# One product of a Strassen-style transform, made for two column chunks at once by a second Strassen level

## The chip, the core and the metric

The kernel runs on one core of one Trainium2 chip. A core has five engines with a queue each: TensorE (PE in the profile; its weight loads are listed as PEld), VectorE (DVE), ScalarE (ACT), GpSimd (POOL) and SyncE (SP, which here only starts transfers). Transfers between the chip's main memory (DRAM) and the on-chip memory (SBUF) are started from SP's or POOL's queue and carried by 16 DMA engines. Matmul results go to PSUM, eight banks of 128 partitions by 512 fp32 numbers. The metric is the device time of one execution in microseconds (us).

## The reference

`x` has 2048 rows of 640. It is normalised by row (`xn`), and two branches are made from it: a Fourier mix over both axes, and a gated feed-forward block, whose result gates the mix.

```python
xn = _layernorm(x, axis=-1)
a = jnp.einsum("bsd,ed->bse", xn, dft_hid_re)
b = jnp.einsum("bsd,ed->bse", xn, dft_hid_im)
s = jnp.einsum("ts,bse->bte", dft_seq_re, a) - jnp.einsum("ts,bse->bte", dft_seq_im, b)
g = _silu((_silu(xn @ w_gate) * (xn @ w_up)) @ w_down)
return x + s * g
```

The kernel swaps the order of the two transforms: it first forms `dft_seq_re @ xn` and `dft_seq_im @ xn` (the sequence transform, 2048 x 2048 by 2048 x 640), keeps them in DRAM (`p_dram`), and then applies the hidden transform. The change is in the sequence transform.

## The kernel before

**Precision.** Every matmul operand in fp32 is split into a high part (ScalarE, a copy rounded to the matmul's format) and a low part (VectorE, the difference). `split` (line 328) records both; `mm3` (line 354) makes one product as three matmuls, high by high, high by low and low by high.

**Strassen.** Every large product is done by one level of Strassen's scheme (Winograd's form): the left matrix in four blocks 11, 12, 21, 22, the right in four, seven products p1, p5, p6, p2, p3, p7, p4 instead of eight. The 640 columns of `xn` are 2 x 256 that go through the scheme and 128 more that are multiplied directly; these ride on operands that are there anyway (d1, d2, d3).

**The sequence transform.** `seq(k)` (line 742) is called for k = 0 to 3. k % 2 chooses real or imaginary (`ri`), k // 2 chooses `j`. A part k makes the output's row chunks of 512 numbered j (upper half) and j + 2 (lower half): in the transposed layout that the kernel uses, these are columns, hence "column chunks". So the lower half's chunks 2 and 3 belong to parts j = 0 and j = 1 of the same `ri`. The DFT matrix (`cs`) is the moving operand, 512 wide; sums of blocks of `xn` (`right`, line 642) are the weights, 128 x 128. Each product has a depth of 1024, which is 8 k-tiles, taken in four groups of two (g = 0 to 3). `run` (line 798) makes one product: for two PSUM banks, and for a third one (`dbank`) where a direct product rides along.

Left operands: `load` (line 759) brings a block of 512 KB by SP's queue, `accumulate` (line 765) adds another block onto it during the transfer by POOL's queue, `add` (line 769) adds on VectorE. `result` (line 835) reads a bank pair, adds or subtracts a kept partial result, and sends it to `p_dram` by POOL's queue. Part 0 has its own opening, which makes p1 for parts 0 and 1 at once. The order of the other parts is p1, p2, p5, p6, p3, p7, p4; part 1 starts with p2. The last product is (lines 976 to 985):

```python
run(("p4", p4, (), (2, 3)))
result("d2", (dbank[2],), None, None)
run(("p4", lambda g: last[g], b2, None))
result(21, b2, s1 if shared else None, ALU.add)
```

p4 multiplies block 22 of the DFT matrix with the weight sum nt4 (`right("p4", g, ...)`), and d3 the same block with nt5. Both sums are made once, in part 0, and kept in SBUF until the end of part 3.

**What sets the order.** The kernel doesn't issue as it goes: every operation is recorded in a plan (`Plan`, line 98), which gives the matmul steps fixed times (`step`, 0.22667 us per matmul), then evictions behind them (`post`), and sets everything that prepares operands (`prod`) backwards from its due time into the free time of its engine. The issue order of each engine is the order of these planned times. Then `place` (line 197) gives every buffer an address in one of three areas of SBUF: `hl` (split operands, 86 KB per partition), `raw` (unsplit data, 80 KB) and a third that is turned over later (20 KB). A buffer may reuse space only of one that is done by the issue order; `fit` (line 247) prefers space that has been free for some time, and takes less (`pauses`) where there is none. All waits between engines follow from the buffers. In the profile all instructions bear line 82, the recording helper, so they are told apart by their operands and shapes.

After the sequence transform come `hid_s` (hidden transform), `gate_up` and `down` (feed-forward).

Of the kernel before, what the change touches and what calls it, by code (L numbers as in the profile page):

```python
# [11 lines left out]
AF = mybir.ActivationFunctionType  # L12
ALU = mybir.AluOpType

P = 128
S, D, F = 2048, 640, 1536
TC = 512
# [80 lines left out]
class Plan:  # L98
# [98 lines left out]
    def place(self, limits, last):  # L197


        self.ops.sort(key=lambda o: o[:2])  # L200
        life = {}
        for i, (t, _, _, names, end) in enumerate(self.ops):
            for n in names:
                if n in self.size:
                    v = life.setdefault(n, [t, i, end, i])
                    v[2:] = max(end, v[2]), i
        where = {}
        turn = max(v[3] for n, v in life.items() if self.size[n][0] == "raw2")
        free = max(v[2] for n, v in life.items() if self.size[n][0] == "raw2")
        back = next(i for i, o in enumerate(self.ops) if o[0] >= self.back)  # L210
        for arena, limit in limits.items():
            wall = {"hl": [(limit, limit + last[0], turn, free + 1, 1e9), (limit + last[0], limit + sum(last), turn, free + 1, back)],
                    "raw": [(limit, limit + last[1], back, self.back + 2, 1e9)]}.get(arena, [])
            limit = max([limit, *(w[1] for w in wall)])
            mine = [(n, self.size[n][1], *v) for n, v in life.items() if self.size[n][0] == arena]
            orders = (
                lambda m: (m[2], m[3]),
                lambda m: (m[4] - m[2] < 60, m[2], m[3]),
                lambda m: (m[4] - m[2] < 60, -m[1], m[3]),
                lambda m: (-m[1], m[3]),  # L220
                lambda m: (m[2] - m[4], m[3]),
            )
            pauses = (8, 6, 4, 3, 2, 1, 0, -1, -2, -4, -8)
            tries = ((pauses[a:], o) for a in range(len(pauses)) for o in orders)
            found = [f for f in (self.fit(sorted(mine, key=o), limit, p, wall) for p, o in tries) if f]
            for long, w in [(x, y) for x in (40, 60, 80) for y in (50, 70, 100, 140)]:
                order = sorted(mine, key=lambda m: (m[4] - m[2] < long, m[2] - m[1] / w, m[3]))
                found += [f for f in (self.fit(order, limit, pauses[a:], wall) for a in range(6)) if f]
            for w in range(25, 425, 25) if not found else ():
                order = sorted(mine, key=lambda m: (m[4] - m[2] < 60, m[2] < w, m[2], m[3]))  # L230
                found += [f for f in (self.fit(order, limit, pauses[a:], wall) for a in range(len(pauses))) if f]
            if not found:
                raise ValueError(f"{arena}: no room")
            best = min(found, key=lambda f: f[0])
# [12 lines left out]
    @staticmethod  # L247
    def fit(mine, limit, pauses, wall):

        placed, where, cost = [], {}, {}  # L250
        for n, size, ta, ia, tb, ib in mine:
            near = sorted((o, e, xa, ja, xb, jb) for o, e, xa, ja, xb, jb in placed
                          if (ja <= ib and ia <= jb) or (xa < tb + 8 and ta < xb + 8))
            near += [(a, a if i < ia and t < ta and ib < j else e, ta, ia, tb, ib) for a, e, i, t, j in wall]
            near.sort()
            for pause in pauses:
                gaps, at = [], 0
                for o, e, xa, ja, xb, jb in near:
                    if (ja <= ib and ia <= jb) or (xa < tb + pause and ta < xb + pause):
                        if o - at >= size:  # L260
                            gaps.append((o - at, at))
                        at = max(at, e)
                if limit - at >= size:
                    gaps.append((limit - at, at))
                if gaps:
                    break
            else:
                return None
            o = min(gaps)[1]
            where[n] = o  # L270
            for a, e, xa, ja, xb, jb in near:
                if a < o + size and o < e:
                    cost[n] = cost.get(n, 0.0) + max(0.0, 5 - (ta - xb if ta >= xa else xa - tb)) ** 2
            placed.append((o, o + size, ta, ia, tb, ib))
        return sum(cost.values()), where, cost, mine
# [3 lines left out]
def tile_fnet_swiglu(  # L279
# [97 lines left out]
    def wide(ap):  # L377
        return ap.rearrange("p (a b) -> p a b", b=TC)
# [258 lines left out]


    p_dram = dram.tile([2, NC, ND, P, TC], F32, name="p_dram")
    sums = {}  # L640

    def right(p, g, lead):


        def quad(h, c, w=256):
            k = 8 * h + 4 * g
            return (lambda a=0, n=4: xn_tiles(k + a, n, 256 * c, w)), [(xn, i, c) for i in range(k, k + 4)]

        def new(what, a, b, op, w=256):
            if (what, g) not in sums:  # L650
                name = pl.buf((what, g), "raw", 4 * w)
                view = lambda a=0, n=4: raw(name).rearrange("p (a b) -> p a b", b=w)[:, a:a + n]
                pl.prod(lead, lambda: nc.vector.tensor_tensor(view(), a[0](), b[0](), op=op), [*a[1], *b[1]], [(name, 0)])
                sums[what, g] = view, [(name, 0)]
            return sums[what, g]

        if p == "p1":
            return quad(0, 0)
        if p == "p2":
            return quad(1, 0)  # L660
        if p == "p3":
            return quad(1, 1)
        if p == "p5":
            return new("nt1", quad(0, 0), quad(0, 1), ALU.subtract)
# [12 lines left out]
        return quad(int(p[1]) - 1, 2, P)  # L677
# [64 lines left out]
    def seq(k):  # L742
# [26 lines left out]
        def add(dst, src, lead):  # L769
            pl.prod(lead, lambda: nc.vector.tensor_tensor(raw(dst), raw(dst), raw(src), op=ALU.add),  # L770
                    [(src, 0)], [(dst, 0)])
# [171 lines left out]
            return s  # L943

        def p3(g):
            add(R[g], load(12, g, 20), 12)
            return operand("p3", g, R[g])

        def product_2():
            run(("p2", p2, b1, (1, 2)))  # L950
            result(11, b1, s1, ALU.subtract)
            result("d1", (dbank[1],), ahead["d1"] if shared else None, ALU.add)

        if fresh:
            opening()
        elif not shared:
            run(("p1", p1, b2, (1, 1)))
        s1 = ahead["s1"] if shared else copy("s1", b2)
        if not fresh:
            product_2()  # L960
        run(("p5", p5, b3, (2, 1)))
        n5 = copy("n5", b3)
        if fresh:
            product_2()
        run(("p6", p6, b2, None))
        if shared:
            u2 = pl.buf(("u2", k), "raw", 2 * TC)
# [5 lines left out]
        result(12, b3, u2, ALU.subtract)  # L973
        run(("p7", lambda g: operand("p7", g, Y[g]), b2, None))
        result(22, b2, n5, ALU.subtract)
        last = []

        def p4(g):
            last.append(operand("p4", g, load(22, g, 20)))
            return last[-1]  # L980

        run(("p4", p4, (), (2, 3)))
        result("d2", (dbank[2],), None, None)
        run(("p4", lambda g: last[g], b2, None))
        result(21, b2, s1 if shared else None, ALU.add)

    seq.n = 0


# [435 lines left out]
```

## Time and profile before

| | |
|---|---|
| median of 3 runs | 969.31 us (969.18 to 969.34) |
| profiled execution: span from first to last instruction | 967.6 us |
| its time outside the span | not listed; the median is 1.7 us above the span |
| TensorE busy | 961.5 us (99%) |
| VectorE busy | 734.5 us (76%) |
| ScalarE busy | 488.8 us (51%) |
| moved by transfers | 186.50 MB, mean 193 GB/s |
| mean granted TensorE clock | 0.999 |

How to read it: busy times are sums of an engine's instructions. Matmuls are pipelined, so a matmul's record is longer than the distance between two of them. A row of a group of instructions has line, engine, operation, output <- input, shapes, count, then busy time and mean ns of one, then the idle time of the engine just ahead of these instructions and what ended it. `hl` are split operands, `raw` unsplit data, `ps` PSUM, `xn` the normalised rows, `in_cs` the DFT matrix. The clock is given in parts of full speed. By the counts of matmuls (132 for the opening with its weights and 360 for the rest of part 0, 360 for part 1, 432 each for parts 2 and 3) part 0 ends at some 121.7 us, part 1 at 203.4, part 2 at 301.4 and part 3 at 399.4 us.

### The profile page before, as it was taken

To read this page: it belongs to the slowest core of one execution; us is meant where nothing else is said; L and a number is where in the kernel's file an instruction comes from. 1 tells how busy PE (TensorE), PEld (TensorE's weight loads), DVE (VectorE), ACT (ScalarE), POOL (GpSimd) and SP (SyncE) were. 2 spreads that over 40 slices of the span, in tenths; PEclk is the share of its full clock that TensorE was granted. 3 is DMA by queue.
4 is the path that set the end of the run, shared out by engine and by line. 5 is a ranking of instruction groups with operands and counts; after the bars stand their busy time and mean duration, and the time that the engine had idled before them with its cause. 6 is when DMAs were issued, how large, how long until landed. Compare 5 with 4: busy or idle time off the path is not lost.

```text
span 967.6 us, 11522 instructions
## 1 busy us (share of the span) xinstructions
PE 961.5 (99%) x4235; PEld 792.1 (82%) x4235; DVE 734.5 (76%) x932; ACT 488.8 (51%) x676; POOL 121.4 (13%) x185
## 2 busy tenths in 40 slices
PE   9999999999999999999999999999999999999998
PEld 5888888888888888888888888888888888888886
DVE  7889668757774687675987898999978666666775
ACT  6686445454545455544356555563446444444341
POOL 0450211011101110111100211210002000000000
PEclk9999999999999999999999999999999999999999
DMA  9997848484838497778563374449799330105793
GB/s 344 280 259 215 227 154 233 150 270 111 226 109 260 108 235 263 204 198 258 165 210 131 142 264 155 168 142 289 219 293 272 80 136 1 55 1 163 243 346 128
DMA packets 64056, 186.50 MB, mean 193 GB/s; under 512 B 6528, under 2 KB 10368, under 8 KB 64000
## 3 DMA queue, kind: packets, MB, share of 16 engines
q1 hardware_dynamic: 45952, 125.45, 39.2%
q0 software_dynamic: 18048, 60.32, 24.0%
q8 instruction: 33, 0.54, 0.2%
q14 instruction: 23, 0.19, 0.1%
HBM read 151.39 MB, written 34.36 MB: 192 GB/s over the span
## 4 chain that ended last, share of the span: by engine, by line
PE 99%; DVE 0%; DMA 0%; ACT 0%; issue 0%; DVEq 0%; ACTq 0%
PE ps L82 99%; DMA xn<-in_x 0%; DVE raw L82 0%; DVE bst L82 0%; DVE sm L82 0%; ACT raw L82 0%; ACT sm L82 0%; DVE mv L82 0%; DVEq L82 0%; ACTq L82 0%
## 5 line engine op out<-in xcount | busy, mean ns | idle before, releaser
L82 PE MATMUL ps<-hl 128*128 128x512 f32 (+1 forms) x3258 | 779.8, 388 | 0.0
L82 PEld LDWEIGHTS ps<-hl 128*128 128x128 f32 x3258 | 610.0, 188 | 126.4 <-ACT hl L82 0.2
L82 DVE TENSOR_TENSOR hl<-raw,hl 128x1024 fp32r<-128x1024 f32 (+5 forms) x360 | 346.6, 994 | 134.5 <-ACT hl L82 94.8
L82 ACT ACTIVATE hl<-raw 128x1024 fp32r<-128x1024 f32 (+6 forms) x416 | 325.1, 826 | 170.6 <-DVE raw L82 84.1
L82 PE MATMUL ps<-hl,hl 128*128 128x512 f32 (+1 forms) x954 | 259.9, 388 | 0.0
L82 ACT ACTIVATE raw<-ps 128x512 f32<-128x512 f32 (+1 forms) x144 | 98.0, 681 | 231.1 <-PE ps L82 225.0
L82 PEld LDWEIGHTS ps<-hl,hl 128*128 128x128 f32 x954 | 178.9, 188 | 36.9
L82 DVE TENSOR_TENSOR raw<-raw 128x1024 f32<-128x1024 f32 (+7 forms) x216 | 178.7, 850 | 19.6 <-ACT raw L82 15.4
L82 DVE TENSOR_TENSOR raw<-ps,raw 128x512 f32<-128x512 f32 (+1 forms) x95 | 77.3, 814 | 48.5 <-PE ps L82 47.7
L82 ACT ACTIVATE hl<-xn 128x1024 fp32r<-128x1024 f32 (+3 forms) x61 | 42.2, 724 | 13.7 <-PE ps L82 9.2
L82 DVE TENSOR_TENSOR raw<-raw,raw 128x512 f32<-128x512 f32 (+3 forms) x50 | 44.2, 892 | 6.5 <-ACT raw L82 4.3
L82 POOL DMA_DIRECT2D p_dram<-raw x24 | 16.4, 687 | 251.5 <-DVE raw L82 215.9
L82 ACT ACTIVATE raw<-raw 128x512 f32<-128x512 f32 (+1 forms) x30 | 21.6, 719 | 46.7 <-DVE raw L82 46.7
L82 DVE TENSOR_TENSOR hl<-xn,hl 128x1024 fp32r<-128x1024 f32 (+3 forms) x50 | 40.8, 833 | 4.0 <-PE ps L82 3.9
L82 POOL DMA_DIRECT2D raw<-in_cs x36 | 32.5, 985 | 57.6 <-DMA raw<-in_cs 28.7
L82 DVE SCALAR_TENSOR_TENSOR hl<-raw,hl 128x256 fp32r<-128x256 f32 (+4 forms) x56 | 32.8, 587 | 4.0 <-ACT hl L82 4.0
L82 POOL DMA_DIRECT2D out<-raw x10 | 6.9, 691 | 225.0 <-DVE raw L82 198.2
L82 POOL DMA_DIRECT2D d_p<-hl x28 | 15.2, 544 | 71.3 <-ACT hl L82 59.2
L82 ACT ACTIVATE xn<-xn,sm,rowst 128x640 f32<-128x640 f32 (+1 forms) x16 | 14.2, 909 | 4.9 <-DVE sm L82 1.8
L82 DVE BATCH_NORM_STATS2 bst<-xn 128x6 f32<-128x320 f32 x32 | 13.7, 479 | 3.6 <-DMA xn<-in_x 3.6
L82 POOL DMA_DIRECT2D y_dram<-raw x12 | 8.2, 684 | 64.6 <-DVE raw L82 46.2
L82 POOL DMA_DIRECT2D raw<-in_xt x6 | 6.9, 1297 | 72.1 <-DVE raw L82 72.1
(43 smaller groups left out, 88.0 us busy)
## 6 DMA issues: line engine op xcount, KB each, us to landing
raw<-in_cs SPq DMA_DIRECT2D x84, 512.0 KB, 7.3
hl<-d_p SPq DMA_DIRECT2D x56, 384.0 KB, 4.7
raw<-in_cs POOLq DMA_DIRECT2D x36, 512.0 KB, 9.8
raw<-in_wb SPq DMA_DIRECT2D x24, 640.0 KB, 4.6
d_p<-hl POOLq DMA_DIRECT2D x28, 384.0 KB, 3.9
p_dram<-raw POOLq DMA_DIRECT2D x16, 512.0 KB, 4.1
raw<-p_dram SPq DMA_DIRECT2D x8, 768.0 KB, 8.2
xn<-in_x SPq DMA_DIRECT2D x16, 320.0 KB, 9.8
```

Source lines behind the costliest of these rows:

```text
L82: return real(*args, **kw)
```

## The change

Parts 0 and 1 (j = 0) no longer make p4 and d3. They keep what p7 leaves in its bank pair (U3, two banks; in part 1 with s1 added) and the direct sum (D2, one bank) in SBUF. Parts 2 and 3 (j = 1) make p2 first, then `second()`, then p1, p5, p6, p3 and p7, without a p4.

`second()` makes p4 and d3 for chunks 2 and 3 of one `ri` together: block 22 of both chunks is one matrix of depth 1024 by 1024 columns, and nt4 is 1024 by 256. It is cut in four again and multiplied by seven products of depth 512 (4 k-tiles), one bank each, in the order p1, p5, p6, p2, p3, p7, p4. The direct products d1 (beside p1 and p5), d2 (beside p2) and d3 (beside p4) ride along as before. Its weights are sums of nt4's blocks (l1 to l4) and of nt5's (e, l6); its left operands are loaded by SP (`take`), added to by accumulating transfers of POOL (`grow`) and by one addition on VectorE (for p6). Chunk 2's results Z1, Z2 and Z5 are finished here from U3 and D2 and sent to `p_dram`; chunk 3's stay as W1 and in the bank `dbank[2]`, and are added in when part 2 or 3 ends.

nt4 and nt5 are made anew in parts 2 and 3 and no longer kept from part 0. In part 1 p3's left operand is added to by an accumulating transfer instead of a load and an addition. The search for buffer addresses gets a further way of ordering, used where the others find no room.

The diff, cut to its core:

```diff
 (Plan.place)
+            for o in orders if not found else ():
+                for p in (-2, 1, 3):
+                    order = sorted(mine, key=o)
+                    for _ in range(200):
+                        f = self.fit(order, limit, [x for x in pauses if x <= p or x > 5], wall)
+                        if f:
+                            found.append(f)
+                            break
+                        i = next(i for i, m in enumerate(order) if m[0] == Plan.stuck)
+                        order.insert(i // 2, order.pop(i))
...
 (right)
-                name = pl.buf((what, g), "raw", 4 * w)
+                name = pl.buf((what, g, len(turn)), "raw", 4 * w)
...
 (seq)
         def p3(g):
-            add(R[g], load(12, g, 20), 12)
+            if shared:
+                accumulate(R[g], 12, g, 14)
+            else:
+                add(R[g], load(12, g, 20), 12)
             return operand("p3", g, R[g])
...
+        def second():
+            q1, (q2, q3), d0 = b2[0], b3, b2[1]
+            Y, R = {}, {}
+            for what in [w for w in sums if w[0] in ("nt4", "nt5")]:
+                del sums[what]
+            turn.append(k)
+            nt = [right("p4", b, 16) for b in range(2)]
+            e = [right("d3", b, 16) for b in range(2)]
...
+            def grow(name, a, b, g, lead):
+                pl.prod(lead, lambda: nc.gpsimd.dma_start(wide(raw(name)), block(a, b, g), accum_op=ALU.add),
+                        [], [(name, 0), (name, 1)], 8)
...
+            def left(p, g):
+                if p == "p1":
+                    Y[g] = take(0, 0, g, 24)
+                    return Y[g]
+                if p == "p5":
+                    R[g] = take(1, 0, g, 30)
+                    grow(R[g], 1, 1, g, 22)
+                    return R[g]
+                if p == "p6":
+                    add(R[g], Y[g], 12)
+                    return R[g]
+                if p == "p2":
+                    return take(0, 1, g, 20)
+                if p == "p3":
+                    grow(R[g], 0, 1, g, 14)
+                    return R[g]
+                return Y[g] if p == "p7" else take(1, 1, g, 20)
+
+            def weights(p):
+                dst = pl.buf(("V", k, p), "hl", 8 * P)
+                src, keys = T2[p]
+                split(11, dst, 4 * P, src, keys, scale=-1.0 if p == "p1" else None, low_lead=9)
+                return dst
+
+            mix("l1", q(0, 0), q(0, 1), ALU.subtract)
+            mix("l2", q(1, 1), l["l1"], ALU.add)
+            mix("l3", q(0, 1), q(1, 1), ALU.subtract, q(0, 1))
+            mix("l4", q(1, 0), l["l2"], ALU.subtract)
+            mix("l6", e[1], e[0], ALU.subtract)
...
+            def phase(p, bank, direct=None):
...
+                for g in range(2):
+                    if (p, g) not in ops2:
+                        name = left(p, g)
+                        ops2[p, g] = o = pl.buf(("S2", k, p, g), "hl", 4 * TC)
+                        split(10, o, 2 * TC, lambda name=name: raw(name), [(name, 0), (name, 1)], low_lead=8)
+                        if p == "p6":
+                            grow(Y[g], 1, 0, g, 11.5)
...
+                    for r, bk in t[::-1]:
+                        for i in range(2):
+                            steps.append((bk, lambda part, r=r, a=2 * g + i: hl(made2[r], part, a * P, P),
+                                          lambda part, o=ops2[p, g], i=i: hl(o, part, i * TC, TC), is_first(bk)))
...
+            phase("p1", q2, ("d1", d0))
+            v1 = less("v1", q2, U3[ri], 0)
+            phase("p5", q3, ("d1", dbank[2]))
+            m5 = pl.buf(("m5", k), "raw", TC)
+            evict(m5, (q3,))
+            phase("p6", q2)
+            v2 = less("v2", q2, U3[ri], TC)
+            phase("p2", q1, ("d2", d0))
+            out(less("Z1", q1, v1, 0), 0, 1)
+            out(less("Z5", d0, D2[ri], 0, ALU.add), 4, 1)
+            phase("p3", q3)
+            out(less("Z2", q3, v2, 0), 1, 1)
+            phase("p7", q2)
+            W1 = pl.buf(("W1", k), "raw", 2 * TC)
+            pl.post(lambda: nc.vector.tensor_tensor(raw(W1, TC, TC), ps[:, q2, :], raw(m5), op=ALU.subtract),
+                    [("ps", q2), (m5, 0)], [(W1, 0)])
+            phase("p4", q2, ("d3", dbank[2]))
+            pl.post(lambda: nc.scalar.activation(raw(W1, 0, TC), ps[:, q2, :], AF.Copy), [("ps", q2)], [(W1, 0)])
...
         if fresh:
             opening()
-        elif not shared:
+        else:
+            run(("p2", p2, b1, (1, 2)))
+        if j:
+            W1 = second()
             run(("p1", p1, b2, (1, 1)))
...
+        if not j:
+            D2[ri] = pl.buf(("D2", ri), "raw", TC)
+            evict(D2[ri], (dbank[2],), after=1)
         run(("p6", p6, b2, None))
...
         run(("p7", lambda g: operand("p7", g, Y[g]), b2, None))
         result(22, b2, n5, ALU.subtract)
-        run(("p4", p4, (), (2, 3)))
-        result("d2", (dbank[2],), None, None)
-        run(("p4", lambda g: last[g], b2, None))
-        result(21, b2, s1 if shared else None, ALU.add)
+        if j:
+            result("d2", (dbank[2],), None, None)
+            result(21, b2, W1, ALU.add)
+            return
+        U3[ri] = pl.buf(("U3", ri), "raw", 2 * TC)
+        if shared:
+            combine(U3[ri], b2, s1, ALU.add, after=3)
+        else:
+            evict(U3[ri], b2, after=3)
```

More of the change, by code (lines that the diff above doesn't have):

```diff
@@ L267, in fit @@
             else:
+                Plan.stuck = n
                 return None
@@ L639, in tile_fnet_swiglu @@
     p_dram = dram.tile([2, NC, ND, P, TC], F32, name="p_dram")
-    sums = {}
+    sums, turn = {}, []
     def right(p, g, lead):
@@ L945, in p3, with block, take, mix @@
         def p3(g):
-            add(R[g], load(12, g, 20), 12)
+            if shared:
+                accumulate(R[g], 12, g, 14)
+            else:
+                add(R[g], load(12, g, 20), 12)
             return operand("p3", g, R[g])
-        def product_2():
-            run(("p2", p2, b1, (1, 2)))
+        def second():
[6 more added lines that the diff above has]
+            e = [right("d3", b, 16) for b in range(2)]
+            q = lambda b, c: (lambda: nt[b][0]()[:, :, c * P:c * P + P], nt[b][1])
+            l = {}
+            def block(a, b, g):
+                return cs[a + 2, ri, 2 + b, :, 2 * g:2 * g + 2]
+            def take(a, b, g, lead):
+                seq.n += 1
+                name = pl.buf(("c", seq.n), "raw", 2 * TC)
+                pl.prod(lead, lambda: nc.sync.dma_start(wide(raw(name)), block(a, b, g)), [], [(name, 0), (name, 1)])
+                return name
+            def grow(name, a, b, g, lead):
+                pl.prod(lead, lambda: nc.gpsimd.dma_start(wide(raw(name)), block(a, b, g), accum_op=ALU.add),
+                        [], [(name, 0), (name, 1)], 8)
+            def mix(what, a, b, op, over=None):
+                if over is None:
+                    name = pl.buf((what, k), "raw", 4 * P)
+                    over = (lambda: raw(name).rearrange("p (a b) -> p a b", b=P)), [(name, 0)]
+                l[what] = over
+                pl.prod(12, lambda: nc.vector.tensor_tensor(over[0](), a[0](), b[0](), op=op), [*a[1], *b[1]], over[1])
+            def left(p, g):
[25 more added lines that the diff above has]
+            mix("l6", e[1], e[0], ALU.subtract)
+            T2 = {"p1": q(0, 0), "p5": l["l1"], "p6": l["l2"], "p2": q(1, 0), "p3": q(1, 1),
+                  "p7": l["l3"], "p4": l["l4"], "d1": e[0], "d2": e[1], "d3": l["l6"]}
+            made2, ops2, todo = {}, {}, []
+            def phase(p, bank, direct=None):
+                t = [(p, bank)] if bank is not None else []
+                if direct:
+                    t.append((direct[0], direct[1]))
+                at = pl.now
+                for g in range(2):
+                    pl.now = at + g * 6 * len(t) * MM
+                    if (p, g) not in ops2:
[4 more added lines that the diff above has]
+                            grow(Y[g], 1, 0, g, 11.5)
+                    for r, _ in t:
+                        if r not in made2:
+                            made2[r] = weights(r)
+                pl.now = at
+                for g in range(2):
+                    steps, reads = [], []
+                    for r, bk in t[::-1]:
+                        for i in range(2):
+                            steps.append((bk, lambda part, r=r, a=2 * g + i: hl(made2[r], part, a * P, P),
+                                          lambda part, o=ops2[p, g], i=i: hl(o, part, i * TC, TC), is_first(bk)))
+                    for r, _ in t:
+                        reads += both(made2[r])
+                    product(steps, list(dict.fromkeys(both(ops2[p, g]) + reads)))
+            def out(name, e0, n):
+                pl.post(lambda: nc.gpsimd.dma_start(p_dram[ri, 2, e0:e0 + n].rearrange("k p t -> p k t"), wide(raw(name))),
+                        [(name, 0)], [("pd", ri, 2)], 5, 8)
+            def less(what, bank, other, a, op=ALU.subtract):
+                name = pl.buf((what, k), "raw", TC)
+                pl.post(lambda: nc.vector.tensor_tensor(raw(name), ps[:, bank, :], raw(other, a, TC), op=op),
+                        [("ps", bank), (other, 0)], [(name, 0)])
+                return name
+            phase("p1", q2, ("d1", d0))
[16 more added lines that the diff above has]
+            pl.post(lambda: nc.scalar.activation(raw(W1, 0, TC), ps[:, q2, :], AF.Copy), [("ps", q2)], [(W1, 0)])
+            for bank in (q1, q2, q3, d0):
+                first.pop(bank)
+            return W1
@@ L951, in product_2, with result_1 @@
+        def result_1():
             result(11, b1, s1, ALU.subtract)
@@ L959, in seq @@
         if not fresh:
-            product_2()
+            result_1()
         run(("p5", p5, b3, (2, 1)))
@@ L963, in seq @@
         if fresh:
-            product_2()
+            run(("p2", p2, b1, (1, 2)))
+            result_1()
+        if not j:
+            D2[ri] = pl.buf(("D2", ri), "raw", TC)
+            evict(D2[ri], (dbank[2],), after=1)
         run(("p6", p6, b2, None))
@@ L975, in seq @@
         result(22, b2, n5, ALU.subtract)
[L976 to L980, printed above, removed]
-        run(("p4", p4, (), (2, 3)))
-        result("d2", (dbank[2],), None, None)
-        run(("p4", lambda g: last[g], b2, None))
-        result(21, b2, s1 if shared else None, ALU.add)
+        if j:
[7 more added lines that the diff above has]
+            evict(U3[ri], b2, after=3)
+    U3, D2 = {}, {}
     seq.n = 0
```

## The prediction

> **What bounds the kernel now.** The page's head was read first, then the chain of work that ended last in order of time, then the groups of instructions by form.
>
> ```profile
> span 967.6 us, 11522 instructions
> PE 961.5 (99%) x4235; PEld 792.1 (82%) x4235; DVE 734.5 (76%) x932; ACT 488.8 (51%) x676; POOL 121.4 (13%) x185
> ...
> PEclk9999999999999999999999999999999999999999
> ```
> ```profile
> 6.30 0.04 issue
> 6.34 956.68 PE ps L82 x4224
> ```
> ```profile
> L82 PE MATMUL ps<-hl 128*128 128x512 f32 x3228 | 775.4, 389 | 0.0
> ...
> L82 PE MATMUL ps<-hl,hl 128*128 128x512 f32 x948 | 258.4, 389 | 0.0
> ...
> L82 PE MATMUL ps<-hl 128*128 128x256 f32 x30 | 4.4, 283 | 0.0
> ...
> L82 PE MATMUL ps<-hl,hl 128*128 128x256 f32 x6 | 1.7, 282 | 0.0
> ```
> ```profile
> L82 PE MATMUL ps<-hl x3258: 278/389/796, 11.5 to 962.6; 128*128 128x512 f32 x190, 128*128 128x256 f32 x2
> L82 PE MATMUL ps<-hl,hl x954: 279/389/397, 383.2 to 962.7; 128*128 128x512 f32 x190, 128*128 128x256 f32 x1
> ```
>
> The chain is one piece: from 6.34 us on, 956.68 us of TensorE without a break, and the idle column of all four matmul groups is 0.0. The kernel is its number of matmuls times their pace. The pace: 3258 + 954 = 4212 matmuls start between 11.5 and 962.7 us; 36 of them (30 + 6) are 256 wide and count half, so 4194 in 951.2 us, or **0.2268 us each** (the 389 ns of a record overlap the next one). The sum below is made against this execution, whose span is 967.6 us; the median of the runs, 969.31 us, is 1.7 us more, which lies around the span and which the change doesn't touch. So what is taken from the span is taken from the median.
>
> **The change: TensorE.** Before, each of the four parts (row and column side of two column chunks, k = 0 to 3) makes p4 with 8 k-tiles x 2 banks x 3 = 48 matmuls and d3 with 8 x 1 x 3 = 24, so 72; four times, 288. After, parts 0 and 1 have neither. Parts 2 and 3 have `second()`: seven products of 4 k-tiles x 1 bank x 3 = 12, and four direct ones (d1 beside p1 and p5, d2 beside p2, d3 beside p4) of 12, so 132; twice, 264. That is **24 matmuls fewer: 24 x 0.2268 = 5.44 us**. Their forms are unchanged (128 x 128 weights, 512 columns), so the pace holds, as long as each of the 132 finds its operands. 969.31 - 5.44 = 963.87 us is the floor.
>
> **The change: VectorE and ScalarE.** All of their work is prepared ahead of the matmuls by the planner, so what counts is whether it can be.
>
> ```profile
> L82 DVE TENSOR_TENSOR hl<-raw,hl 128x1024 fp32r<-128x1024 f32 x162 | 194.0, 1221 | 77.9 <-ACT hl L82 48.2 <-issue 23.9 <-PE ps L82 5.1
> ...
> L82 ACT ACTIVATE hl<-raw 128x1024 fp32r<-128x1024 f32 x162 | 166.5, 1053 | 120.6 <-PE ps L82 55.4 <-DVE raw L82 51.2 <-issue 4.8
> ...
> L82 DVE TENSOR_TENSOR raw<-raw 128x1024 f32<-128x1024 f32 x60 | 72.4, 1220 | 3.5 <-DMA raw<-in_cs 2.2 <-ACT raw L82 0.7
> L82 ACT ACTIVATE raw<-ps 128x512 f32<-128x512 f32 x113 | 67.5, 598 | 160.7 <-PE ps L82 155.0 <-DVE raw L82 2.3 <-ACT hl L82 1.9
> ...
> L82 DVE TENSOR_TENSOR raw<-ps,raw 128x512 f32<-128x512 f32 x73 | 50.5, 691 | 28.2 <-PE ps L82 27.4
> ...
> L82 DVE TENSOR_TENSOR raw<-ps,raw 128x1024 f32<-128x1024 f32 x22 | 26.9, 1222 | 20.3 <-PE ps L82 20.3
> ...
> L82 DVE TENSOR_TENSOR raw<-raw 128x512 f32<-128x512 f32 x37 | 25.6, 691 | 14.0 <-ACT raw L82 12.7
> ...
> L82 DVE TENSOR_TENSOR hl<-raw,hl 128x512 fp32r<-128x512 f32 x14 | 9.6, 685 | 0.0
> ...
> L82 ACT ACTIVATE hl<-raw 128x512 fp32r<-128x512 f32 x14 | 8.7, 620 | 1.7 <-DVE raw L82 1.3 <-DMA raw<-in_cs 0.4
> L82 DVE TENSOR_TENSOR raw<-xn,raw 128x1024 f32<-128x1024 f32 x4 | 4.9, 1220 | 0.2 <-ACT xn L82 0.2
> ```
>
> Taken away in each part: p4's four operand splits, two splits of its weights, two of d3's. On VectorE 6 x 1.221 + 2 x 0.685 = 8.70 us, on ScalarE 6 x 1.053 + 2 x 0.620 = 7.56. In part 1 p3's four additions (4 x 1.220 = 4.88 us) become accumulating transfers. Added in each `second()`, on VectorE: nt4 2 x 1.220, nt5 2 x 0.691, the five mixed sums 5 x 0.691, ten weight splits 10 x 0.685, fourteen operand splits 14 x 1.221, p6's additions 2 x 1.220, six readings of PSUM (v1, v2, Z1, Z5, Z2 and W1's upper half) 6 x 0.691: 2.44 + 1.38 + 3.46 + 6.85 + 17.09 + 2.44 + 4.15 = **37.8 us, while its 132 matmuls last 29.9**. ScalarE: 14 x 1.053 + 10 x 0.620 + 2 x 0.598 = 22.1 us, which fits. U3 and D2 take the same reading of PSUM that 21 and d2 had in parts 0 and 1. At the end of parts 2 and 3 21 is read with W1 by VectorE (1.22) instead of copied out by ScalarE.
>
> So 7.9 us of VectorE work per pass must be done ahead. Nothing of it hangs on a matmul but the six readings; nt4, nt5 and the mixed sums (7.3 us) need only space. The products on both sides, p2 before and p1 after, last 72 x 0.2268 = 16.3 us each and have 8.7 us of such work each. Over the three, VectorE has 55.2 us (some 57 with the previous part's last results) in 276 x 0.2268 = 62.6 us: 91%. Can the kernel run so? The busy times by stage (columns: window, length, PE, PEld, DVE, ACT, POOL, clock, DMA share, GB/s) answer it; the part edges follow from the matmul counts.
>
> ```profile
> 48.00:72.00 24.00, 24.00 (x107) 19.89 (x106) 20.66 (x32) 19.99 (x26) 14.58 (x28) 1.00 0.99 261
> 72.00:96.00 24.00, 24.00 (x107) 19.88 (x106) 23.95 (x24) 14.87 (x17) 1.36 (x2) 1.00 0.74 215
> 672.00:696.00 24.00, 24.00 (x107) 19.89 (x106) 23.86 (x20) 8.55 (x8) 0.00 (x0) 1.00 0.84 296
> ```
> ```profile
> 105.40:121.70 16.30, 16.30 (x74) 13.49 (x73) 8.14 (x10) 7.56 (x9) 4.59 (x6) 1.00 0.97 263
> ...
> 203.40:301.40 98.00, 98.00 (x434) 81.14 (x433) 67.58 (x61) 49.39 (x53) 11.22 (x14) 1.00 0.64 178
> 301.40:399.40 98.00, 98.00 (x434) 81.15 (x433) 67.48 (x59) 52.00 (x54) 13.77 (x16) 1.00 0.77 218
> ```
>
> From 72 to 96 us VectorE is busy 23.95 of 24 us, at 672 again 23.86, and TensorE never pauses. Part 2 as a whole goes from 67.58 to 67.6 - 8.7 + 37.8 + 1.2 = 97.9 us in 98.0 + 60 x 0.2268 = 111.6 us, 88%. So I cost VectorE at nothing, hidden by the 13.7 us in which it is then still idle in each of these parts; without that cover it is 7.9 us a pass. Parts 0 and 1 lose the p4 stage, here at 105.4 to 121.7 us, in which VectorE worked 8.14 of 16.3 us: about what p4 itself asked for (8.70), so no catching up is lost.
>
> **The change: transfers.** For part 2 as it is (queue rows: packets, MB, share of the window; issue rows: count, size, median us to landing):
>
> ```profile
> q1 hardware_dynamic: 2909, 10.59, 33.6%
> q0 software_dynamic: 1888, 6.82, 30.6%
> ...
> raw<-in_cs SPq DMA_DIRECT2D x20, 512.0 KB, 7.0
> raw<-in_cs POOLq DMA_DIRECT2D x8, 512.0 KB, 9.4
> p_dram<-raw POOLq DMA_DIRECT2D x4, 512.0 KB, 4.3
> p_dram<-raw POOLq DMA_DIRECT2D x2, 256.0 KB, 6.5
> ```
>
> A load keeps the transfer engines 0.336 x 98 / 20 = 1.65 us. With the stores (five times 512 KB) at that rate, an accumulating load takes (0.306 x 98 - 5 x 1.65) / 8 = 2.7 us. Each pass has 8 loads, 6 accumulating ones and 768 KB of stores: 13.2 + 16.2 + 2.5 = 31.9 us for 29.9 us of matmuls; p4's four loads (6.6 us) go. In part 1 four loads become accumulating ones (+4.2 us), and p4's loads and chunk 2's stores go. Part 2 comes to 62.7 - 6.6 + 31.9 = 88.0 of 111.6 us (79%), part 3 to 75.5 + 25.3 = 100.8 (90%). From 48 to 72 us the share was 0.99 and nothing stalled, so this too is costed at nothing, with prefetch into p2's stage as the cover. The Trainium skill ("DMA: Bandwidth & Descriptors", section "Issuing engines are not separate DMA queues") says that transfers started by different engines run on the same 16 DMA engines and interleave. The profile agrees in that it counts both queues on the same 16 engines (33.6 + 30.6 = 64, the window's 0.64). By this rule the pass is 2.0 us short, which is rival 1; were POOL's queue a set of its own, 13.2 us would stand on SP's side, 18.7 on POOL's, and nothing would be short.
>
> The queues are in order. On SP the eight loads wait for raw space, and p1's four loads stand behind them. On POOL, p3's accumulation onto R waits for p6's splits of R; the stores of Z1, Z5, Z2 and the later p5's accumulations stand behind it. Chunk 2's stores move from parts 0 and 1 into parts 2 and 3. Their reader, the hidden transform, starts at part 3's end: after the last of them 36 matmuls of `second()` and 288 of the part follow, 73 us, against a landing of 6.5.
>
> **The one new tight wait.** p7 and p4 share bank q2: W1's upper half must be read between them, with only d3's first six matmuls as cover.
>
> ```profile
> 529.66 0.62 PE L82 MATMUL ps<-hl,hl 128*128 128x512 f32 x2
> ...
> 530.32 0.69 DVE L82 TENSOR_TENSOR raw<-ps,raw 128x512 f32<-128x512 f32 x1 [0.21 <-PE ps L82]
> ```
>
> A reading starts 0.04 us after the matmul's end at 530.28, lasts 0.69, and an issue takes 0.04 more: 0.77 us. The cover is 6 x 0.227 less the overlap of the records (0.389 - 0.227 = 0.16), 1.20 us. If VectorE is free there is no stall (0); if it has just begun a split of 1.22, p4 starts 0.77 + 1.22 - 1.20 = 0.8 us late, and all of TensorE behind it. I take 0.25 of it per pass, since the planner reserves VectorE at that time: 0.5 us in all. The other reuses have 24 matmuls or more (5.4 us) between writer and reader. The new placement search has no instruction of its own; reuse of space could delay operands (below nothing is excluded, no wait being on the path now), and that belongs to the rivals.
>
> Sum: 969.31 - 5.44 + 0.5 = **964.4 us** (-0.5%).
>
> **Rivals.**
>
> 1. *Transfers become the bound of `second()`.* Place: R's second accumulation. After p6's split it takes 9.4 to land and 1.05 + 1.22 to split, 11.7 us, while p6 and p2 last 36 x 0.2268 = 8.2; p6's operands must stand 3.5 us early. For it: the pass's 31.9 us against 29.9, and the waits of SP's queue, which are for space:
>
> ```profile
> SPq L82 <- DVE raw L82: 282.4, 32, 42.9
> SPq L82 <- DVE hl L82: 249.1, 37, 24.5
> ```
>
> Against it: p2's stage, with four loads in 16.3 us. Price if nothing is ahead: 2.0 us a pass, 963.9 + 4.0 = 967.9 us, no change that a measurement tells; all 3.5 us of the chain would be 970.9.
>
> 2. *VectorE becomes the bound (slower).* Place: p6 to p4, where products of 12 matmuls (2.72 us) each want 2 x 1.221 + 0.685 = 3.13 us of splits besides readings. If none of the 7.9 us is done ahead, 963.9 + 15.8 = 979.7 us; if half, 971.8. It decides above 3.7 us a pass (2 x 3.7 = 5.4 + 1.9). For it: ScalarE's splits already wait 55.4 us for operand space that matmuls free, so running ahead has a limit. Against it: the 23.95 us row. The Trainium skill ("TensorE: Matmul & The Clock Gate", "HAM oscillation — how this bites in real kernels") adds that a pause of TensorE above some 3.4 us halves its clock; no window here shows one (clock 1.00), and the estimate from that page is up to 1.7 us more per such pause.
>
> 3. *The matmuls saved are given to another gap*, the order of parts 0 and 1 losing cover at 105.4 us, where the transfer share is 0.97: 16.3 us of stage hold 15.8 us of transfers, of which p4's loads and chunk 2's stores are 6.6 + 2.5. The other 6.7 must go elsewhere; all on the path would be 970.6 us. Against it: part 1's own share is lower.
>
> **Numbers.** Forecast 964.4: 0.68 (its own range 963.6 to 966.5). Rival 1: 0.13, rival 2: 0.12, rival 3: 0.07. A measurement can tell 0.2%, 1.94 us, from no change. Faster: the forecast and 0.05 of rival 1: 0.73. Same: 0.08 of rival 1, 0.05 of rival 3: 0.13. Slower: rival 2 and 0.02 of rival 3: 0.14. The range 963.5 to 970.0 leaves out rival 2 and a little more.
>
> **What would show it.** 4188 matmuls beside the 12 of the opening and 11 of the warm-up; in the chain a TensorE piece of 951 us; idle columns of the matmul groups near 0.0, with less than 1 us put down to VectorE on `ps`. Rival 1 shows as TensorE waiting for ScalarE or VectorE on `hl` while these wait for `raw<-in_cs`; rival 2 as the same with VectorE at 24 of 24 us through `second()`; rival 3 as gaps at 105 to 125 us. I am wrong if the matmuls are 24 fewer and the span isn't 2.8 us shorter.

## The result

The changed kernel takes **963.74 us** (median of 5 runs, 963.56 to 963.83), the kernel before 969.31 (969.18 to 969.41): a ratio of 0.9942, 95% interval 0.993 to 0.9954. Forecast were 964.4 us and, as the floor without any gap, 963.87. The kernel sits on the floor: 0.13 us below it, which is within the spread of the runs.

The page's head and the chain of work that ended last, changed kernel:

```profile
span 962.0 us, 11593 instructions
PE 955.9 (99%) x4211; PEld 787.6 (82%) x4211; DVE 765.1 (80%) x976; ACT 499.1 (52%) x694; POOL 136.1 (14%) x203
```
```profile
6.45 0.04 issue
6.50 951.02 PE ps L82 x4200
```

The TensorE piece is still one, with 4200 matmuls instead of 4224, and 951.02 us instead of 956.68. The span is 5.6 us shorter (967.6 to 962.0), the runs 5.57. Nothing took the place of what was saved. Groups of matmuls by form (busy, mean ns, then idle time ahead of them): two rows, both without idle time.

```profile
L82 PE MATMUL ps<-hl 128*128 128x512 f32 x3210 | 793.4, 389 | 0.0
...
L82 PE MATMUL ps<-hl,hl 128*128 128x512 f32 x942 | 279.0, 389 | 0.0
```

By the matmul counts part 2 now begins at 170.7 us. Its stages p2, second level (the pass), p1, then the whole of parts 2 and 3 (columns as in the prediction's windows: window, length, PE, PEld, DVE, ACT, POOL, clock, DMA share, GB/s):

```profile
170.70:187.00 16.30, 16.30 (x74) 13.50 (x73) 16.21 (x19) 7.44 (x9) 2.50 (x3) 1.00 0.93 237
187.00:217.00 30.00, 30.00 (x134) 24.85 (x133) 23.06 (x28) 15.27 (x20) 6.96 (x9) 1.00 0.99 272
217.00:233.30 16.30, 16.30 (x73) 13.51 (x72) 13.27 (x12) 10.92 (x13) 0.00 (x0) 1.00 0.50 124
...
170.70:282.30 111.60, 111.60 (x494) 92.42 (x493) 93.89 (x95) 62.63 (x71) 16.92 (x21) 1.00 0.77 204
282.30:393.90 111.60, 111.60 (x494) 92.45 (x493) 89.36 (x89) 62.31 (x70) 18.87 (x23) 1.00 0.86 243
```

Here the cover can be seen. In p2's stage VectorE is busy 16.21 of 16.3 us, where p2 itself wants 8.7, some of it done earlier, and two readings of part 1's results take 2.4: what remains is work for the pass. In the pass it then has 6.9 us to spare. The transfer engines are at 0.93 and 0.99 of their time. Both engines that rivals 1 and 2 named are thus close to full somewhere in these 46 us, and TensorE notices neither. So the open questions were how far the gain hangs on matmuls alone, and how much more of VectorE and of transfers this stage would bear.

### The profile page after: what moved, and what is told of

Same layout as the page of the kernel before. It is cut to its first block, busy times and chain, and to the rows that moved or that the text cites. A ratio compares the mean times of both kernels' runs of the same rounds, so it can differ in the third digit from the quotient of the medians.

```text
span 962.0 us, 11593 instructions
## 1 busy us (share of the span) xinstructions
PE 955.9 (99%) x4211; PEld 787.6 (82%) x4211; DVE 765.1 (80%) x976; ACT 499.1 (52%) x694; POOL 136.1 (14%) x203
## 4 chain that ended last, share of the span: by engine, by line
PE 99%; DMA 0%; DVE 0%; ACT 0%; issue 0%; ACTq 0%; DVEq 0%
PE ps L82 99%; DMA xn<-in_x 0%; DVE raw L82 0%; DVE bst L82 0%; DVE sm L82 0%; ACT raw L82 0%; ACT sm L82 0%; DVE mv L82 0%; ACTq L82 0%; DVEq L82 0%
## 5 line engine op out<-in xcount | busy, mean ns | idle before, releaser
L82 PE MATMUL ps<-hl 128*128 128x512 f32 x3234 | 797.5, 388 | 0.0
L82 DVE TENSOR_TENSOR hl<-raw,hl 128x1024 fp32r<-128x1024 f32 (+5 forms) x374 | 358.5, 989 | 98.7 <-ACT hl L82 77.0
L82 ACT ACTIVATE hl<-raw 128x1024 fp32r<-128x1024 f32 (+7 forms) x432 | 336.0, 822 | 180.6 <-DVE raw L82 91.4
L82 PE MATMUL ps<-hl,hl 128*128 128x512 f32 x954 | 281.1, 388 | 0.0
L82 DVE TENSOR_TENSOR raw<-raw 128x1024 f32<-128x1024 f32 (+6 forms) x230 | 189.0, 843 | 17.3 <-ACT raw L82 14.6
L82 DVE TENSOR_TENSOR raw<-ps,raw 128x512 f32<-128x512 f32 (+1 forms) x109 | 87.7, 808 | 51.9 <-PE ps L82 49.0
L82 POOL DMA_DIRECT2D raw<-in_cs x52 | 46.2, 990 | 130.6 <-DVE hl L82 54.0
L82 DVE SCALAR_TENSOR_TENSOR hl<-raw,hl 128x256 fp32r<-128x256 f32 (+5 forms) x58 | 34.2, 591 | 3.9 <-ACT hl L82 3.8
L82 POOL DMA_DIRECT2D raw<-p_dram x8 | 10.1, 1260 | 55.7 <-DVE raw L82 32.9
L82 DVE BATCH_NORM_STATS2 bst<-xn 128x6 f32<-128x320 f32 x32 | 13.7, 480 | 3.8 <-DMA xn<-in_x 3.8
```

The costliest lines, as they stand in the source:

```text
L82: return real(*args, **kw)
```

## The experiments

In each, the kernel before ran on the same chip beside it (969.29 to 969.39 us). The theory is the prediction's: the time is the number of matmuls times 0.2268 us, as long as everything else is ready in time. The rivals are that the gain has another source, and that VectorE, the transfers or the wait between p7 and p4 are at their limit.

### The order alone

Made from the kernel before:

```diff
-        elif not shared:
+        else:
+            run(("p2", p2, b1, (1, 2)))
+        if j:
             run(("p1", p1, b2, (1, 1)))
...
         if not fresh:
-            product_2()
+            result_1()
...
```

> The kernel before with one thing moved: parts 2 and 3 make p2 ahead of p1, as the changed kernel does; no second level. 4212 matmuls as before. Theory (time is the number of matmuls times 0.2268 us, all else is hidden): 969.3 us, the same as before. Rival (the new order itself gives or costs time): more than 1 us off 969.3, in part 2 or 3, with idle time of TensorE to show for it.

Measured: 969.37 us (969.28 to 969.56), ratio 1.0 (0.9991 to 1.001). Its chain:

```profile
6.44 956.50 PE ps L82 x4224
```

4224 matmuls (4212 and the 12 of the opening) in the same time. Moving p2 ahead of p1 gives and costs nothing.

### One side alone

Made from the changed kernel; where the last lines are left out, p4, d3 and their results stand as in the kernel before:

```diff
+        two = ri == 0
+        if j and two:
+            W1 = second()
         if j:
-            W1 = second()
             run(("p1", p1, b2, (1, 1)))
...
-        if not j:
+        if not j and two:
...
+        if not two:
...
+            return
```

> The change for the real side alone (parts 0 and 2); the imaginary side (parts 1 and 3) makes p4 and d3 as before, with nt4 and nt5 made anew. 12 matmuls fewer than before. Theory: half of the saving, 969.3 - 12 x 0.2268 = 966.6 us. Rival (the gain comes from the shorter first parts or the transfers that they no longer make, not from matmuls): anything but the half, 963.7 or 969.3 us.

Measured: 966.32 us (966.02 to 966.69), 2.97 below the kernel before beside it, with the theory's 966.6 inside the spread of its runs.

```profile
6.34 953.86 PE ps L82 x4212
```

12 matmuls fewer, 2.8 us less in the chain. Half of the change gives half of the gain. By itself this doesn't tell the matmuls from the shorter first parts, since the run has half of both. The chains do: in all four kernels TensorE is one unbroken piece, so nothing else can have been waited for there, and its pace is the same, 0.2264 to 0.2265 us per matmul (956.68 / 4224, 956.50 / 4224, 953.86 / 4212, 951.02 / 4200).

### The wait between p7 and p4, without its cover

```diff
-                    for r, bk in t[::-1]:
+                    for r, bk in (t if p == "p4" else t[::-1]):
```

> In the second level's last phase p4's matmuls go ahead of d3's, in each of the two steps, so that nothing lies between p7's last matmul and p4's first on the same bank. Theory of the prediction's tight wait: each pass then waits for the reading of the bank, 0.04 + 0.69 + 0.04 us and the 0.16 us by which records overlap, 0.93 us if VectorE is free, up to 1.22 more if a split has just begun: 963.7 + 1.9 = 965.6 us, at most 968.0. Rival (the six matmuls of d3 cover nothing, the reading is over sooner or waits for something else): 963.7 us.

Measured: 965.97 us (965.84 to 966.17), 2.23 above the changed kernel. The chain, in order of time, now breaks once in each pass:

```profile
6.42 205.57 PE ps L82 x894
211.99 0.02 issue
212.02 0.70 DVE raw L82
212.72 0.14 issue
212.85 111.78 PE ps L82 x492
324.63 0.02 issue
324.66 0.70 DVE raw L82
325.36 0.14 issue
325.49 634.27 PE ps L82 x2814
```

The wait is what the prediction said: reading of the bank 0.70 us, with 0.02 ahead and 0.14 behind it (0.04 and 0.04 were forecast), and the 0.16 of overlapping records: 1.02 us a pass, 2.04 of the 2.23 us. So the six matmuls of d3 do cover something, and in the changed kernel they cover all of it. Why no stall at all remains there shows in VectorE's timeline of the changed kernel:

```profile
209.90 1.22 DVE L82 TENSOR_TENSOR hl<-raw,hl 128x1024 fp32r<-128x1024 f32 x1
212.01 0.69 DVE L82 TENSOR_TENSOR raw<-ps,raw 128x512 f32<-128x512 f32 x1 [0.90 <-PE ps L82]
212.62 1.22 DVE L82 SCALAR_TENSOR_TENSOR hl<-xn,hl 128x1024 fp32r<-128x1024 f32 x1
```

VectorE has been idle for 0.90 us, waiting for p7, when the reading starts. No split stands in its way.

### More work for VectorE

The low halves of the pass's operands are made twice, all 14 or the first of each product's two. The doubling happens at issue, so addresses and order stay those of the changed kernel.

```diff
             if scale is None:
-                nc.vector.tensor_tensor(lo, src(), hi, op=ALU.subtract)
+                for _ in range(1 if nc.dry else again):
+                    nc.vector.tensor_tensor(lo, src(), hi, op=ALU.subtract)
...
+                        split(10, o, 2 * TC, lambda name=name: raw(name), [(name, 0), (name, 1)], low_lead=8, again=2)
```

> The changed kernel with every low half of the second level's 14 operands per pass made twice, the plan unaware of it: the same placement, the same order, 14 x 1.221 = 17.1 us more of VectorE per pass. In the changed kernel VectorE is idle for 6.9 of the pass's 30.0 us, and the plan leaves 2.5 us between an operand and its matmul. Theory (VectorE's cover is what keeps the pass without gaps): 17.1 - 6.9 - 2.5 = 7.7 us of gaps per pass, 963.7 + 15.4 = 979 us, from 975 to 985; the clock drops if single gaps get long. Rival (operands are ready long before they are due, the cover is much deeper than the idle time): 963.7 to 966 us.

Measured: 990.36 us (989.85 to 990.96), 26.6 above the changed kernel, more than the theory's 975 to 985. TensorE's timeline in the first pass, with the idle time ahead of each piece in brackets:

```profile
192.16 19.11 PE L82 MATMUL ps<-hl 128*128 128x512 f32 x83 [1.53 <-DVE hl L82]
212.03 1.94 PE L82 MATMUL ps<-hl 128*128 128x512 f32 x7 [0.76 <-DVE raw L82]
214.93 1.65 PE L82 MATMUL ps<-hl 128*128 128x512 f32 x6 [0.96 <-DVE hl L82]
217.32 0.50 PE L82 MATMUL ps<-hl 128*128 128x512 f32 x1 [0.74 <-DVE hl L82]
218.53 1.20 PE L82 MATMUL ps<-hl 128*128 128x512 f32 x4 [0.70 <-DVE hl L82]
224.45 20.79 PE L82 MATMUL ps<-hl 128*128 128x512 f32 x81 [4.73 <-DVE raw L82]
```

Six gaps, 9.4 us, and 1.0 us for the overlap that is lost six times: 10.4 of the 13.3 us a pass. Most of the rest is the clock. Windows around the long gap:

```profile
216.00:219.70 3.70, 2.26 (x8) 1.02 (x6) 3.67 (x7) 0.00 (x0) 0.33 (x1) 1.00 0.43 153
219.70:224.45 4.75, 0.02 (x2) 0.00 (x1) 4.71 (x6) 0.00 (x0) 3.19 (x5) 0.76 0.94 248
224.45:226.00 1.55, 1.55 (x4) 1.26 (x5) 1.55 (x2) 0.00 (x0) 0.00 (x0) 0.50 0.95 159
...
227.50:229.00 1.50, 1.50 (x5) 1.11 (x5) 0.00 (x0) 0.00 (x0) 0.00 (x0) 0.50 0.96 377
229.00:231.00 2.00, 2.00 (x10) 1.64 (x9) 0.00 (x0) 0.01 (x1) 0.88 (x1) 1.00 1.09 322
```

After a pause of 4.73 us the granted clock is 0.50 for some 4.6 us, which costs 2.3 us of matmuls (after the same pause in the second pass 3.3 us, which costs 1.6); the five pauses of up to 1.53 us left it at 1.00. That agrees with the rule of the Trainium skill that the prediction named ("TensorE: Matmul & The Clock Gate", "HAM oscillation — how this bites in real kernels": pauses above some 3.4 us halve the clock). As a lower limit the 3.4 us doesn't hold here: under "More transfers" a pause of 2.72 us is followed by half the clock.

The theory had taken 2.5 us of the plan's reserve off the gaps. 17.1 us more of VectorE, less the 10.4 us of delay, leave 6.7: the idle 6.9 us alone, and no reserve besides. The smaller dose was to tell whether that reading holds:

> As the run with 14 low halves made twice, but only the first of each product's two operands: 7 x 1.221 = 8.5 us more of VectorE per pass, the plan unaware. The 14 cost 13.3 us per pass, of which 9.4 were gaps. Theory A (only VectorE's idle 6.9 us of the pass are cover, the plan's 2.5 us have been used up by then): 8.5 - 6.9 = 1.6 us per pass, no pause long enough for the clock, 963.7 + 3.2 = 967 us. Theory B (the 2.5 us still stand): 963.7 to 964.2 us. Theory C (each microsecond more of VectorE costs one, there is no cover): 963.7 + 17 = 981 us.

Measured: 968.9 us (967.95 to 969.75), 5.2 above the changed kernel, 2.6 a pass, where theory A had 1.6. B and C fall. The median hides two groups: five runs took 967.95 to 968.28 us, the other five 969.53 to 969.75 at a mean clock of 0.998 instead of 0.999 to 1.000. The trace is of the first group (968.09); why the others took 1.5 us more stays open, a lower clock after the pauses being the likely cause. In the trace each pass has a single gap (2.27 us, in the second pass 1.50), and not ahead of an operand:

```profile
215.56 24.82 PE L82 MATMUL ps<-hl 128*128 128x512 f32 x108 [2.27 <-DVE raw L82]
```

TensorE has all its operands; it waits for `raw` written from the bank, which is W1's upper half. VectorE's timeline of the same run:

```profile
213.69 1.22 DVE L82 TENSOR_TENSOR hl<-raw,hl 128x1024 fp32r<-128x1024 f32 x1
214.82 0.68 DVE L82 TENSOR_TENSOR raw<-ps,raw 128x512 f32<-128x512 f32 x1
215.42 1.22 DVE L82 SCALAR_TENSOR_TENSOR hl<-xn,hl 128x1024 fp32r<-128x1024 f32 x1
```

The reading runs at 214.82 instead of 212.01, behind a late split. New theory: VectorE's lag doesn't reach TensorE through the operands, which are still ahead, but through the one reading that TensorE waits for, since it stands in the same in-order queue.

### The same reading on ScalarE

```diff
-            pl.post(lambda: nc.vector.tensor_tensor(raw(W1, TC, TC), ps[:, q2, :], raw(m5), op=ALU.subtract),
...
+                    nc.scalar.activation(raw(W1, TC, TC), ps[:, q2, :], AF.Copy)
...
+            def lower():
+                nc.scalar.activation(raw(W1, 0, TC), ps[:, q2, :], AF.Copy)
+                if not nc.dry:
+                    nc.vector.tensor_tensor(raw(W1, TC, TC), raw(W1, TC, TC), raw(m5), op=ALU.subtract)
...
```

> The changed kernel, but the bank between p7 and p4 (W1's upper half) is read by a plain copy on ScalarE, and VectorE subtracts m5 after p4, off TensorE's path; the plan is unaware. Both theories below: 963.7 us, since TensorE waits for nothing in the changed kernel.

Measured: 964.06 us (963.82 to 964.33). As expected, no gain, since nothing was waited for.

> The same reading on ScalarE, with 7 low halves per pass made twice as in the run of 968.9 us. There the one gap per pass, 2.27 us, stood between p7 and p4 at the reading of the bank, queued on VectorE behind late splits. Theory (VectorE's lag reaches TensorE first through this reading, the operands themselves being still ahead): the gap goes, 963.7 to 965 us. Rival (VectorE is out of time, the next operand would be as late as the reading): 968.9 us again.

Measured: **964.02 us** (963.96 to 964.22), against 968.9 (967.95 in the lowest run) with the reading on VectorE. The chain is whole again, and VectorE is as busy in the pass as in the run with the gap. The row of the pass with the reading on VectorE, then the chain and that row with it on ScalarE:

```profile
187.00:217.00 30.00, 27.73 (x122) 22.62 (x122) 29.81 (x35) 17.49 (x22) 6.97 (x9) 1.00 0.93 247
```
```profile
6.50 951.00 PE ps L82 x4200
```
```profile
187.00:217.00 30.00, 30.00 (x134) 24.83 (x133) 29.81 (x35) 18.07 (x23) 6.96 (x9) 1.00 0.93 251
```

VectorE has 29.81 busy of 30.0 us in both; TensorE has a gap in one and none in the other. The new theory holds, and theory A falls as it was put: the 6.9 idle us are not what decided. VectorE can be out of idle time in this pass without a loss; it was the position of one 0.69 us reading in its queue.

> The same reading on ScalarE, with all 14 low halves made twice as in the run of 990.4 us. There each pass had gaps of 1.53, 0.76, 0.96, 0.74 and 0.70 us ahead of operands or banks and one of 4.73 at the reading between p7 and p4, after which the clock stood at half for some 4 us. Theory: the five short gaps stay (4.7 us a pass and 0.16 each for the overlap), the long one shrinks and the clock with it: 963.7 + 2 x 5.5 = 975 us, from 973 to 982. Rival (the lag is the same wherever it is met): 987 to 990 us.

Measured: 977.65 us (977.43 to 977.88), in the theory's range. The first five gaps of the first pass stay as they were (1.53, 0.77, 0.96, 0.73 and 0.71 us); this is the sixth, in TensorE's timeline, and the pass's window:

```profile
221.60 13.69 PE L82 MATMUL ps<-hl 128*128 128x512 f32 x59 [0.80 <-DVE hl L82]
```
```profile
187.00:217.00 30.00, 26.01 (x111) 20.14 (x109) 29.69 (x31) 15.66 (x21) 3.47 (x4) 1.00 0.78 199
```

It is 0.80 us ahead of an operand instead of 4.73 at the reading, 5.5 us of gaps in this pass (4.8 in the second), and the clock is 1.00. With 17 us more VectorE is the bound after all; the reading and the clock that fell with it made the other 12.7 of the 26.6 us.

### More transfers

```diff
-                pl.prod(lead, lambda: nc.sync.dma_start(wide(raw(name)), block(a, b, g)), [], [(name, 0), (name, 1)])
...
+                    for f in far if not nc.dry else ():
+                        nc.sync.dma_start(f, block(a, b, g))
+                    nc.sync.dma_start(wide(raw(name)), block(a, b, g))
...
```

> The changed kernel with four more transfers per pass, unknown to the plan: ahead of the first of the two loads of p1, p5, p2 and p4 in the second level the same 512 KB are copied within main memory, to a place that nobody reads, on SP's queue. At a load's rate 4 x 1.65 = 6.6 us of the transfer engines, at most double that. In the changed kernel their share from 170.7 to 217 us is 0.97, 1.4 us idle. Theory (the transfers have no room in the pass, and loads arrive just in time): 6.6 - 1.4 - 2.5 = 2.7 us per pass, 969 us, from 965 to 982. Rival (loads are far enough ahead, or p2's stage takes it): 963.7 us.

Measured: 964.05 us (963.96 to 964.24).

> The same with a copy ahead of each of the eight loads: 13.2 us more per pass. Theory (no room): 13.2 - 1.4 - 2.5 = 9.3 us per pass and pauses long enough for the clock, 963.7 + 18.6 = 982 us, up to 1010 if a copy within main memory takes the engines twice as long as a load. Rival (prefetch covers it): 963.7 to 965 us.

Measured: 963.73 us (963.7 to 963.94). The theory falls in both: the rival's number was right. Part 1, p2's stage and the pass with eight copies more:

```profile
105.40:170.70 65.30, 65.30 (x289) 54.07 (x289) 53.35 (x49) 34.84 (x38) 13.28 (x17) 1.00 0.82 213
170.70:187.00 16.30, 16.30 (x73) 13.49 (x73) 16.22 (x19) 7.45 (x10) 2.50 (x3) 1.00 0.98 286
187.00:217.00 30.00, 30.00 (x134) 24.82 (x134) 22.95 (x28) 14.84 (x20) 5.54 (x8) 1.00 1.03 303
```

The share of the transfer engines goes from 0.93 to 0.98 in p2's stage and from 0.99 to 1.03 in the pass, part 1 takes some as well (0.76 to 0.82), and no matmul waits. Between 105 and 233 us the eight copies add 7.9 us of busy time, 1.0 us each (the second pass's eight some 1.3 each, by the same shares from 233 to 394 us): less than the 1.65 that a load was put at, so the dose was smaller than stated.

> The changed kernel with four copies within main memory ahead of each of the second level's eight loads, 32 per pass instead of the 8 that changed nothing. The 8 added 7.9 us of busy transfer engines between 105 and 233 us, 1.0 us each; in the changed kernel some 17 us of the 82 us before the pass are free. Theory (the transfers do have a limit, 8 us of it is cover): 32 - 17 = 15 us a pass too many, less what waiting hides, 970 to 995 us, with ScalarE waiting for loads. Rival (copies and loads don't compete): 963.7 us.

Measured: 1036.26 us (1033.73 to 1037.63), far above the theory's 995. Here the transfers are the bound, with a share of 1.00 from 170.7 to 217 us. TensorE's timeline in the first pass, and ScalarE's own wait there:

```profile
198.37 1.22 PE L82 MATMUL ps<-hl 128*128 128x512 f32 x2 [10.92 <-ACT hl L82]
...
225.99 17.64 PE L82 MATMUL ps<-hl 128*128 128x512 f32 x66 [6.52 <-DVE raw L82]
```
```profile
ACT hl L82 <- DMA raw<-in_cs: 61.4, 8, 28.7
```

ScalarE waits 61.4 us for loads; the copies stand ahead of them in SP's in-order queue and take 19.2 us (median) to land. The direction of the theory holds, its size doesn't: I reckoned with free engine time and not with the order of the queue, and the pauses of 10.92 and 6.52 us bring the clock down too (0.60 in the pass). How the 36 us a pass divide was not taken further. The limit lies between 8 and 32 copies. In the second pass a shorter pause is enough for the clock, 2.72 us ahead of the matmul at 366.52 (TensorE's timeline, then windows):

```profile
366.52 7.42 PE L82 MATMUL ps<-hl 128*128 128x512 f32 x24 [2.72 <-DVE raw L82]
```
```profile
366.50:367.60 1.10, 1.08 (x4) 0.78 (x5) 1.10 (x3) 0.00 (x0) 0.00 (x0) 1.00 1.08 272
367.60:371.00 3.40, 3.40 (x10) 2.61 (x9) 0.57 (x1) 0.00 (x0) 0.00 (x0) 0.50 1.02 359
```

### p3's accumulation undone

```diff
-            if shared:
-                accumulate(R[g], 12, g, 14)
-            else:
-                add(R[g], load(12, g, 20), 12)
+            add(R[g], load(12, g, 20), 12)
...
```

> The changed kernel with one part undone: in part 1 p3's left operand is made by a load and an addition on VectorE again (four loads and 4.9 us of VectorE for four accumulating transfers); the address search has more ways to try, since the one in the change finds no room for this. Theory (what lies beside the matmuls costs nothing while it is ready in time; this part of the change is there for space): 963.7 us. Rival (VectorE's 4.9 us were needed in the shortened part 1): gaps in part 1, 964.7 us or more.

Measured: 963.59 us (963.42 to 964.11). VectorE is busy 55.44 instead of 53.31 us from 105.4 to 170.7 us, and TensorE doesn't wait (65.30 of 65.30 us). This part of the change is worth no time. That it is there for space is an argument from the address search alone.

## Why the prediction was right

**The floor.** 24 matmuls fewer at 0.2268 us each were to take 5.44 us; the runs show 5.57, and 4200 matmuls stand in the chain (4188 and the 12 of the opening). The half change gave its half, the order alone nothing. The result lies near the lower end of the forecast's own range (963.6 to 966.5).

**VectorE "at nothing".** Right, and a cover was named rightly: p2's stage, one of the two named, is full at 16.21 of 16.3 us. The reason given was weak, though: 13.7 us of idle time in a whole part don't tell what a pass can bear, since 8.5 us more in it cost 5.2 us in all. The size was off too. I summed records, 1.221 us for an operand's low half; back to back they follow closer (in the rows above the split of 213.69 is followed at 214.82, 1.13 us later), and over the kernel the change adds 30.6 us of VectorE where my terms, less 3.8 us for the nt4 and nt5 that part 0 no longer makes (not in the prediction), add up to 34.6. Summed record by record the two traces differ by 35.0 us (786.2 and 821.2), so the terms were right and their overlap was missing. Part 2 has 93.89 us of it instead of 97.9.

**Transfers "at nothing".** Right. Shares of 0.77 and 0.86 in parts 2 and 3 against the reckoned 79% and 90%. Rival 1 is refuted for the load that the change brings, and for eight copies more.

**The tight wait.** The mechanism was right, and its price was seen when the cover was taken away (1.0 us a pass and a little more, forecast 0.93). The 0.5 us in the sum was wrong: nothing is lost, since VectorE idles 0.90 us ahead of the reading. It is also most of the distance between forecast and result (964.4 less 0.5 is 963.9).

**Rival 2** was put at the wrong place. I let VectorE's lag show ahead of operands, from p6 to p4. The runs showed that it shows first at W1's reading, with 8.5 us more work; with the reading on another engine the same work cost 0.3 us in all. I had priced the tight wait with one split ahead of it at most (0.8 us), and VectorE's load apart from it; they are one. The clock's part, estimated in the prediction at up to 1.7 us a pause, was 2.3 and 1.6 us after the two pauses of 4.73 us.

**Rival 3**: no gap at 105 us; the TensorE piece runs through.

## What to carry to other kernels

Where one engine is busy without a break, a change is worth its instructions on that engine times their pace, and the rest is a question of readiness: look for the stage whose cover is thinnest and ask what is queued there, not for the average share. An engine can be full for 30 us beside the bound and cost nothing, as long as what it makes is ahead; a single short instruction that the bound waits for, in the same in-order queue, turns its lag into a stall. Put such readings on a queue that is not backed up, or give them cover from the bound's own work.

## What the hardware showed beside that

In the traces of the runs with doubled low halves, pauses of TensorE of up to 1.53 us and one of 2.27 us left its granted clock at 1.00, and pauses of 4.73 us brought it to 0.50 for 4.6 and 3.3 us after they ended; a pause of 2.72 us in the run with 32 copies was followed by 3.4 us at 0.50. No trace shows why five of the runs with seven low halves doubled had a mean clock of 0.998. The transfer engines' share stood at 0.98 to 1.03 for 46 us with a whole chain of matmuls beside it (eight copies). TensorE wrote a bank that VectorE had read 0.14 us after the reading ended in the run without cover, and 0.06 us after it in those with seven and with 14 low halves doubled (214.82 + 0.68 to 215.56; 223.71 + 0.68 to 224.45); VectorE started 0.02 us after a matmul's end, which the profile models.
